# Row transposes of three chunks by transfers instead of TensorE, with the last steps of a spectral stage regrouped

## Chip, cores and metric

The kernel runs on one core of one Trainium2 chip. The metric is the device time of one execution in microseconds (us), the median of several runs. Before the change it is 183.4 us, the median of three runs between 183.24 and 183.43.

## What is computed

```python
def reference(A_x, A_w_r, A_w_i, B_x, B_w_gate, B_w_up, B_w_down):
    x = A_x                                   # 1 x 2048 x 512, bf16
    xn = _layernorm(x, axis=-1)
    # branch A: a filter in the frequency domain
    #   X = rfft2(xn) * (w_r + 1j*w_i);  y = irfft2(X)
    # branch B: a gated MLP, 512 -> 1792 -> 512
    #   h = gelu(xn @ w_gate) * (xn @ w_up);  z = h @ w_down
    return x + _A_ref(xn, A_w_r, A_w_i) + _B_ref(xn, B_w_gate, B_w_up, B_w_down)
```

B_x is not used. Both branches read the normalised rows xn.

## The kernel before

All work is written out by hand as a list of operations for each engine (PE is TensorE, ACT is ScalarE, DVE is VectorE, POOL is GpSimd, SP is SyncE). `sch.op(engine, fn, deps)` appends one operation; at its place in the list the engine waits for the semaphores in `deps` and goes on. So each engine, SP with its transfers too, works strictly in the order in which the Python code names the operations. Nearly all transfers are issued by SP, on one queue (q1) that is spread over 16 rings; six transfers (`back` with "act") and two early loads are issued by ScalarE on q10.

**Rows.** The 2048 rows are 16 row tiles of 128 (index j), four chunks of four tiles (512 rows). `ln_stats`, `ln_rstd` and `ln_apply` (L402 to L427) normalise a tile into `xn`, which lies in `bufA`. For the MLP the rows are needed transposed. `transposes(a, b, ring)` (L432) does this for tiles a to b-1: 16 transposing matmuls against the identity for a whole chunk (L444), into two PSUM banks, and two evictions into `xnT`, one on VectorE (L451) and one on ScalarE (L453). The first chunk is transposed in two halves before the loops; chunk two right before the loop over j, chunks three and four inside it.

**MLP.** `geglu_unit(b, fc)` ("g", L493) takes row chunk b and one of 14 column tiles: 4 matmuls with w_gate and 4 with w_up (L507), a gelu on ScalarE (L519) and a product on VectorE into `hT` (L527). `down_unit(b, jj)` ("d", L541) is 14 matmuls with w_down (L555) for one row tile, added to x on VectorE (L561). A list `fillers` holds all these units in order; `filler()` puts the next one into the program. They fill TensorE's time between the steps of branch A. Down units of chunk b-1 are put among the g units of chunk b at the positions in L789.

**Spectral branch.** The steps, in the order of the program:
- `half_fold` (POOL, L464) and `mirror_fold` (DVE, L471) form sums and differences of xn in `half` (in `bufC`) and `fold` (in `bufB`).
- Loop over j = 0 to 15 (L823): a filler, `unit_A(j)` (four matmuls, L577), `unit_d(j-1)` (four matmuls, L603). ScalarE evicts `unit_d` into `T[j]` (L611), which lies over `xn` in `bufA`, and SP stores `T[j]` to DRAM `stage_p` (L613; streams dr0 for j under 8, dr1 for the others). The dictionary `beside` names what else is put after each j. The filters wr and wi are loaded by SP at j = 1 and j = 5, ten transfers each (L339).
- `shuffle(q)` (L616): two transfers, SP, that bring half of `stage_p` back into `Tp` (in `bufC`) in another order; they wait for all stores of that half. shuffle(0) stands at j = 10, shuffle(1) after the loop. Every `unit_B` waits for both (`perm1`). `load_eg` (L393) follows, then five fillers.
- Loop over u = 0 to 18 (L842): `unit_c(u-4)`, `unit_B(u)`, `product(u-3)`, a filler. `unit_B` (two matmuls, L649) is evicted by ScalarE into `Xc` (L654), and SP copies it with the halves of the partitions swapped into `JX` (two transfers, L657). `product` (three VectorE operations, L666 to L668) multiplies by the filter. `unit_c` (two matmuls, L680) is evicted by ScalarE into `Vp` (L685), and SP stores it to DRAM `stage_g` (L689). At the end of this loop several c and products come together (L843, L848).
- `back(part, pq, eng)` (L692): transfers that return `stage_g` into `V` (in `bufB`), each waiting for the stores of its part, eight groups. Parts 0 to 2 are issued by ScalarE inside the loop, part 3 by SP after it.
- Five fillers, and a last loop: `unit_e(j)` (L711, needs all of V) evicted into `ZT` (L716, in `bufA`), `unit_fin(j)` (L732), and the sum into x, which SP stores to the output (L539).

The functions that the diff touches follow.

Of the kernel before, what the change touches and what calls it, by code (L numbers as in the profile page):

```python
# [151 lines left out]
class _Sched:  # L152
# [14 lines left out]
    def total(self, stream):  # L167
        return (stream, self.stream_cnt[stream])
# [59 lines left out]
def bass_parallel_sum__spectral_gfnet__glu_gated_geglu__prompt_kernel(  # L228
# [21 lines left out]
    with ExitStack() as es:  # L250
# [34 lines left out]
        xn = bufA[:, :].rearrange("p (j c) -> p j c", j=NJ)  # L285
        T = xn
        ZT = bufA[:, :].rearrange("p (ci j q) -> p ci j q", ci=4, j=NJ)

        fold = bufB[:, :].rearrange("p (t s j d) -> p t s j d", t=2, s=2, j=NJ)
        V = bufB[:, :].rearrange("p (j c) -> p j c", j=NJ)  # L290
# [28 lines left out]
        def sp_bank_bf(slot):  # L319
# [11 lines left out]
        streams += [(n, 16) for n in ("x0", "x1", "x2", "x3", "xc1", "xc2", "xc3", "ident", "small", "fa", "eg", "wd", "wr", "wi",  # L331
                                      "w0", "w1", "w2", "w3", "dr0", "dr1", "perm1", "jx0", "jx1", "jx2", "jx3", "vd0_0", "vd0_1", "vd0_2", "vd1_0", "vd1_1", "vd1_2", "vd2_0", "vd2_1", "vd2_2", "vd3_0", "vd3_1", "vd3_2", "perm2", "out")]
        for name, inc in streams:
# [95 lines left out]
        ev_xnT = {}  # L429
        tr = {}  # L430

        def transposes(a, b, ring, per=2):  # L432
# [23 lines left out]
            for j in range(a, b):  # L456
                ev_xnT[j] = evs
                tr[j] = ev_t

# [137 lines left out]
        def unit_d(j):  # L597
# [12 lines left out]
            src = sp_bank(slot).rearrange("p (h q m) -> p q h m", h=2, q=2)  # L610
            ev_T[j] = sch.op("act", lambda e: e.activation(dst, src, ACT.Copy), deps=[ev_p, tr[j]] + ev_hf[j // 4])  # L611
            ring_sp.add_reader(slot, ev_T[j])
# [92 lines left out]
        def unit_e(j):  # L705
# [9 lines left out]
            src = sp_bank(slot).rearrange("p (ci q) -> p ci q", ci=4)  # L715
            ev_ZT[j] = sch.op("act", lambda e: e.activation(ZT[:, :, j, :], src, ACT.Copy), deps=[ev_p] + [spec["dr%d" % q] for q in range(2)])  # L716
            ring_sp.add_reader(slot, ev_ZT[j])
# [68 lines left out]
        for b in range(4):  # L786
            units = [("g", b, fc) for fc in range(NHALF if b == 0 else 0, NFC)]
            if b >= 1:
                for n, at in enumerate((4, 7, 10, 13) if b < 3 else (3, 5, 7, 14)):  # L789
                    units.insert(at + n, ("d", b - 1, n))  # L790
            fillers += units
# [16 lines left out]
        for j in range(4, 8):  # L808
            ln_apply(j)
        filler(2)  # L810
        transposes(4, 8, ring_tr)
        half_fold(1)
# [4 lines left out]
            4: tuple((ln_apply, i) for i in range(8, 12)) + ((half_fold, 2),),  # L817
            5: ((ln_stats, 12), (ln_stats, 13), (transposes, 8, 12, ring_sp)), 6: ((ln_stats, 14), (mirror_fold, 2, 0)),
            7: ((ln_stats, 15), (ln_rstd, 12, 16), (mirror_fold, 2, 1)),
            8: tuple((ln_apply, i) for i in range(12, 16)) + ((half_fold, 3),), 9: ((transposes, 12, 16, ring_sp),),  # L820
            10: ((mirror_fold, 3, 0), (mirror_fold, 3, 1), (clear_holes,), (shuffle, 0)),
        }
        for j in range(NJ):  # L823
# [18 lines left out]
        for u in range(19):  # L842
            for v in ((14, 15) if u == 18 else (u - 4,)):  # L843
                if v >= 0:
                    unit_c(v)
            if u < 16:
                unit_B(u)
            for v in {16: (13, 14), 17: (15,), 18: ()}.get(u, (u - 3,)):  # L848
                if v >= 0:
                    product(v)  # L850
            if 1 <= u < 18:
                filler()

            if u in (9, 10, 13, 14, 17, 18):
                back(u // 4 - 2, (u - 9) % 4, "act")
        for pq in range(2):
# [61 lines left out]
```

## Time and profile before

| | us |
|---|---|
| median of three runs | 183.4 |
| the profiled execution's own time | 182.99 |
| its span in the profile | 181.2 |
| TensorE busy | 175.1 |
| VectorE busy | 117.3 |
| ScalarE busy | 88.5 |
| GpSimd busy | 55.5 |
| L444, transposing matmuls, 64 of them | 4.4 |
| L451 and L453, their evictions for whole chunks, 3 each | 2.0 and 3.1 |
| L613, the store of T[j], from issue to landing (median of 16) | 7.5 |
| L622, a shuffle transfer of 512 KB, from issue to landing (median of 4) | 5.1 |

The span runs from the first to the last recorded instruction. Busy time is the sum of an engine's instructions; the busy time of pipelined matmuls overlaps (64 transposing matmuls have 4.4 us but take less of the path). The chain of waits goes back from the last instruction, at each step to what released it, so what is on it lies on the path that sets the end. A DMA row gives the mean busy share of the 16 rings in tenths, one digit for each fortieth of the stretch.

### The profile page before, as it was taken

The numbers are of one execution on the slowest core, as the hardware profiler recorded it, in microseconds if no ns is written. First come the engines' busy times: TensorE is split into PE (matmuls) and PEld (weight loads), VectorE is DVE, ScalarE is ACT, GpSimd is POOL, SyncE is SP. The second block draws the span as 40 slices with busy tenths as digits, with TensorE's granted clock in tenths as the row PEclk, the third lists the DMA queues.
The fourth block names the chain that finished last, engine by engine and source line by source line (L and its number), as shares of the span: only waits on it lengthen the run. The fifth ranks groups of instructions, "written<-read, shape, count | busy, mean of one in ns | idle before, by whom it ended". The sixth has DMA issues, their size and how long they took to land.

```text
span 181.2 us, 3176 instructions
## 1 busy us (share of the span) xinstructions
PE 175.1 (97%) x1148; PEld 99.8 (55%) x1168; DVE 117.3 (65%) x252; ACT 88.5 (49%) x161; POOL 55.5 (31%) x54
## 2 busy tenths in 40 slices
PE   7889999999999999999999999999999999999994
PEld 7778555565655554455455554444555555555453
DVE  3758958799675545538678585933266758886431
ACT  2744357777463542166576574523363636663000
POOL 0082290373630000000000000000049679997900
PEclk9999999999999999999999999999999999999999
DMA  5999970999999585723436858475001121110101
GB/s 153 354 364 374 371 250 30 187 195 195 208 205 201 156 257 157 220 58 98 112 87 131 204 113 215 103 168 116 5 0 58 37 75 36 58 60 5 58 29 58
DMA packets 32224, 26.10 MB, mean 144 GB/s; under 512 B 2256, under 2 KB 31440, under 8 KB 32080
## 3 DMA queue, kind: packets, MB, share of 16 engines
q1 hardware_dynamic: 28368, 23.90, 50.2%
q10 hardware_dynamic: 3840, 2.00, 5.3%
q8 instruction: 9, 0.15, 0.4%
q14 instruction: 7, 0.06, 0.1%
HBM read 17.48 MB, written 6.30 MB: 131 GB/s over the span
## 4 chain that ended last, share of the span: by engine, by line
PE 90%; DMA 4%; DVE 3%; SPq 1%; issue 1%
PE ps L507 50%; PE ps L555 27%; DMA wu_sb<-in_B_w_up_dram 4%; PE ps L577 2%; PE ps L732 2%; PE ps L711 2%; PE ps L603 2%; PE ps L649 2%; PE ps L680 2%; PE ps L444 2%; SPq L339 1%; DVE hT L527 1%; DVE tmp L666 1%; DVE tmp L668 0%; DVE JX L667 0%
## 5 line engine op out<-in xcount | busy, mean ns | idle before, releaser
L507 PE MATMUL ps<-xnT,wu_sb 128*128 128x512 bf16 (+1 forms) x246 | 58.3, 358 | 0.1
L507 PE MATMUL ps<-xnT,wg_sb 128*128 128x512 bf16 (+1 forms) x234 | 56.2, 357 | 1.3 <-DMA wu_sb<-in_B_w_up_dram 0.5
L527 DVE TENSOR_TENSOR hT<-ps,gg 128x512 bf16<-128x512 f32 (+1 forms) x62 | 39.5, 638 | 21.7 <-PE ps L507 20.5
L555 PE MATMUL ps<-wd_sb,hT 128*128 128x512 bf16 (+1 forms) x234 | 50.3, 366 | 0.2
L519 ACT ACTIVATE gg<-ps 128x512 bf16<-128x512 f32 (+1 forms) x62 | 34.4, 555 | 25.4 <-PE ps L507 24.3
L746 POOL TENSOR_TENSOR bufC<-bufC 128x256 bf16<-128x256 f32 x16 | 14.7, 917 | 85.5 <-DVE bufC L743 85.5
L507 PEld LDWEIGHTS ps<-xnT,wu_sb 128*128 128x128 bf16 x248 | 24.2, 98 | 24.2
L555 PEld LDWEIGHTS ps<-wd_sb,hT 128*128 128x128 bf16 x238 | 22.9, 98 | 22.6
L507 PEld LDWEIGHTS ps<-xnT,wg_sb 128*128 128x128 bf16 x248 | 22.9, 98 | 16.0 <-DMA wu_sb<-in_B_w_up_dram 0.7
L561 DVE TENSOR_TENSOR x_sb<-ps,x_sb 128x512 bf16<-128x512 f32 (+1 forms) x17 | 11.2, 660 | 28.7 <-PE ps L555 28.7
L750 POOL TENSOR_TENSOR x_sb<-x_sb,bufC 128x512 bf16<-128x512 bf16 x16 | 18.7, 1170 | 2.3
L468 POOL TENSOR_TENSOR bufC<-bufA 128x1024 bf16<-128x1024 bf16 x8 | 16.8, 2125 | 7.9 <-DVE bufA L426 7.9
L611 ACT ACTIVATE bufA<-ps 128x512 bf16<-128x512 f32 x16 | 11.9, 744 | 9.2 <-PE ps L603 9.2
L685 ACT ACTIVATE Vp<-ps 128x514 bf16<-128x514 f32 x16 | 9.6, 599 | 13.6 <-PE ps L680 13.6
L716 ACT ACTIVATE bufA<-ps 128x512 bf16<-128x512 f32 x16 | 9.4, 597 | 13.5 <-PE ps L711 13.5
L403 DVE BATCH_NORM_STATS2 st<-x_sb 128x6 f32<-128x512 bf16 x16 | 10.9, 678 | 2.2 <-DMA x_sb<-in_A_x_dram 2.2
L742 DVE TENSOR_TENSOR bufC<-bufC,ps 128x256 f32<-128x256 f32 x16 | 6.7, 421 | 5.3 <-ACT bufC L739 5.3
L654 ACT ACTIVATE Xc<-ps 128x514 bf16<-128x514 f32 x12 | 7.0, 595 | 4.0 <-PE ps L649 4.0
L418 POOL TENSOR_SCALAR rstd<-ag 128x4 f32<-128x4 f32 (+1 forms) x4 | 1.6, 402 | 20.2 <-DVE ag L404 20.2
L584 ACT ACTIVATE tmp<-ps 128x512 bf16<-128x512 f32 x9 | 5.4, 597 | 4.5 <-PE ps L577 4.5
L739 ACT ACTIVATE bufC<-ps 128x256 f32<-128x256 f32 x16 | 6.0, 378 | 2.6 <-PE ps L732 2.6
L746 DVE TENSOR_TENSOR bufC<-bufC 128x256 bf16<-128x256 f32 x16 | 6.8, 425 | 0.5
(46 smaller groups left out, 144.1 us busy)
## 6 DMA issues: line engine op xcount, KB each, us to landing
stage_g<-Vp SPq DMA_DIRECT2D x16, 128.5 KB, 2.8
stage_p<-bufA SPq DMA_DIRECT2D x16, 128.0 KB, 7.5
bufC<-stage_p SPq DMA_DIRECT2D x4, 512.0 KB, 5.1
out_dram<-x_sb SPq DMA_DIRECT2D x15, 128.0 KB, 1.7
wd_sb<-in_B_w_down_dram SPq DMA_DIRECT2D x1, 1792.0 KB, 14.0
wr_sb<-in_A_w_r_dram SPq DMA_DIRECT2D x6, 257.0 KB, 6.5
wi_sb<-in_A_w_i_dram SPq DMA_DIRECT2D x6, 257.0 KB, 11.0
JX<-Xc SPq DMA_DIRECT2D x24, 64.2 KB, 2.3
```

The lines of the kernel that those rows point to most:

```text
L403: ev = sch.op("dve", lambda e: e.bn_stats(st[:, j, :], x_sb[:, j, :]), deps=[ev_x[j]])
L468: ev_hf[m] = [sch.op("pool", lambda e, t=t, op=op: e.tensor_tensor(half[:, m, t, :, :], rows[:, 0, :, :], rows[:, 1, :, :], op), deps=deps ...
L507: ins = e.matmul(gu_bank(slot)[:, 0:w], wsb[:, dc, fc * P:(fc + 1) * P], xnT[:, dc, b * 512 + a:b * 512 + a + w], start=(dc == 0), stop=(d ...
L519: ev_gg = sch.op("act", lambda e: e.activation(gg, gu_bank(gslot)[:, 0:w], ACT.Gelu_apprx_tanh), deps=[ev_gm] + gg_readers[s2])
L527: ev_h = sch.op("dve", lambda e: e.tensor_tensor(hT[hb][:, fc, a:a + w], gu_bank(uslot)[:, 0:w], gg, ALU.mult), deps=[ev_um, ev_gg] + hdeps)
L555: ins = e.matmul(bank(slot)[:, 0:w], hT[hb][:, fc, jj * P:(jj + 1) * P], wd_sb[:, fc, cs], start=(fc == 0), stop=(fc == NFC - 1))
L561: ev_a = sch.op("dve", lambda e, slot=slot, cs=cs: e.tensor_tensor(x_sb[:, j, cs], bank(slot)[:, 0:w], x_sb[:, j, cs], ALU.add), deps=[ev_ ...
L611: ev_T[j] = sch.op("act", lambda e: e.activation(dst, src, ACT.Copy), deps=[ev_p, tr[j]] + ev_hf[j // 4])
L685: ev_v = sch.op("act", lambda e: e.activation(Vp[sv][:], sp_pair(slot), ACT.Copy), deps=[ev_p] + Vp_readers[sv])
L716: ev_ZT[j] = sch.op("act", lambda e: e.activation(ZT[:, :, j, :], src, ACT.Copy), deps=[ev_p] + [spec["dr%d" % q] for q in range(2)])
L746: y = [sch.op(("dve", "pool")[h], lambda e, h=h, op=op: e.tensor_tensor(rS[s2][:, h * HD:(h + 1) * HD], yeS[s2][:, 0, :], yeS[s2][:, 1, :] ...
L750: ev_o = sch.op("pool", lambda e: e.tensor_tensor(x_sb[:, j, :], x_sb[:, j, :], rS[s2], ALU.add), deps=[a, b, ev_xn[j]] + ev_acc.get(j, []))
```

## The change

Chunks two to four (tiles 4 to 15) are no longer transposed by TensorE. A new `transfers(a, b)` has SP issue one transposing transfer per tile, from `xn` to `xnT`, 12 in all. Those of chunk two stand where their transposes stood; those of chunk three after j = 11, 12, 13 and 14; those of chunk four after u = 2, 4, 6 and 8 of the second loop. Since `xn` is now read later, `T` moves from `bufA` over `fold` in `bufB`, whose layout is turned so that the 512 elements of row tile j lie where `T[j]` is written. `T` no longer waits for the transposes and the half fold, and `ZT` (in `bufA`) waits for the transfers. The last down unit of chunk one moves from position 13 to 11 in the filler list. `product(13)` moves one step earlier (u = 15), 14 and 15 follow singly, `unit_c` 13 and 14 come together at u = 17 and 15 alone at u = 18. The third return (`back` of part 2) moves from u = 17 and 18 to u = 16 and 17.

```diff
-        T = xn
-        fold = bufB[:, :].rearrange("p (t s j d) -> p t s j d", t=2, s=2, j=NJ)
+        fold = bufB[:, :].rearrange("p (j t s d) -> p t s j d", t=2, s=2, j=NJ)
+        T = bufB[:, :].rearrange("p (j c) -> p j c", j=NJ)
...
+        def transfers(a, b):
+            for j in range(a, b):
+                sch.op("sp", lambda e, j=j: e.dma_start(xnT[:, :, j * P:(j + 1) * P], xn[:, j, :], transpose=True),
+                       deps=[ev_xn[j]], stream="tr%d" % (a // 4))
+                ev_xnT[j] = [total("tr%d" % (a // 4))]
+            for i in range(a // 4 * 4, b):
+                ev_xnT[i] = [total("tr%d" % (a // 4))]
...
-            ev_T[j] = sch.op("act", lambda e: e.activation(dst, src, ACT.Copy), deps=[ev_p, tr[j]] + ev_hf[j // 4])
+            ev_T[j] = sch.op("act", lambda e: e.activation(dst, src, ACT.Copy), deps=[ev_p])
...
-            ev_ZT[j] = sch.op("act", ..., deps=[ev_p] + [spec["dr%d" % q] for q in range(2)])
+            ev_ZT[j] = sch.op("act", ..., deps=[ev_p] + [ev_xnT[i][0] for i in (4, 8, 12)])
...
-                for n, at in enumerate((4, 7, 10, 13) if b < 3 else (3, 5, 7, 14)):
+                for n, at in enumerate(((4, 7, 10, 13), (4, 7, 10, 11), (3, 5, 7, 14))[b - 1]):
...
-        transposes(4, 8, ring_tr)
+        transfers(4, 8)
...
-            5: ((ln_stats, 12), (ln_stats, 13), (transposes, 8, 12, ring_sp)), 6: ((ln_stats, 14), (mirror_fold, 2, 0)),
-            7: ((ln_stats, 15), (ln_rstd, 12, 16), (mirror_fold, 2, 1)),
-            8: tuple((ln_apply, i) for i in range(12, 16)) + ((half_fold, 3),), 9: ((transposes, 12, 16, ring_sp),),
+            5: ((ln_stats, 12), (ln_stats, 13)), 6: ((ln_stats, 14), (mirror_fold, 2, 0)),
+            7: ((mirror_fold, 2, 1), (ln_stats, 15), (ln_rstd, 12, 16)),
+            8: tuple((ln_apply, i) for i in range(12, 16)) + ((half_fold, 3),),
...
+            11: ((transfers, 8, 9),), 12: ((transfers, 9, 10),), 13: ((transfers, 10, 11),), 14: ((transfers, 11, 12),),
...
-            for v in ((14, 15) if u == 18 else (u - 4,)):
+            for v in {17: (13, 14), 18: (15,)}.get(u, (u - 4,)):
                 if v >= 0:
                     unit_c(v)
...
-            for v in {16: (13, 14), 17: (15,), 18: ()}.get(u, (u - 3,)):
+            for v in {15: (12, 13), 16: (14,), 17: (15,), 18: ()}.get(u, (u - 3,)):
...
-            if u in (9, 10, 13, 14, 17, 18):
-                back(u // 4 - 2, (u - 9) % 4, "act")
+            if u in (2, 4, 6, 8):
+                transfers(11 + u // 2, 12 + u // 2)
+            if u in (9, 10, 13, 14, 16, 17):
+                back((u - 8) // 4, {16: 0, 17: 1}.get(u, (u - 9) % 4), "act")
```

## Prediction

> **What bounds the kernel now.** I read the page's first part, then the chain of waits in order of time, then the timelines of TensorE and SyncE, then the DMA rows of three stretches. The first two say that TensorE is the path.
>
> ```profile
> PE 175.1 (97%) x1148; PEld 99.8 (55%) x1168; DVE 117.3 (65%) x252; ACT 88.5 (49%) x161; POOL 55.5 (31%) x54
> ...
> PE 90%; DMA 4%; DVE 3%; SPq 1%; issue 1%
> ```
>
> The chain that ended last is 90% TensorE. Until about 10 us it is the loads, and from there to 178.8 us it is matmuls back to back, with one break. From the same chain, in order of time (start, length, what):
>
> ```profile
> 23.97 0.89 PE ps L444 x16
> ...
> 37.68 0.89 PE ps L444 x16
> ...
> 48.74 0.89 PE ps L444 x16
> ...
> 113.34 0.69 DVE hT L527
> ...
> 117.61 0.44 DVE tmp L668
> 118.09 0.40 PE ps L680 x2
> ```
>
> L444 is the transposes of row chunks two to four: three blocks of sixteen, each 0.89 us long, and all three stand on the path. The break is at 113 to 118 us, where the chain leaves TensorE for VectorE: the last two `unit_c` wait for the last two `product`.
>
> **Removed from TensorE.** 48 transposes, 3 x 0.89 = 2.67 us, with matmuls directly before and after each block: **-2.67**. Their evictions go too (three DVE copies of 0.67 us, three ACT copies of 1.02 us). Neither engine is the path there (DVE 65%, ACT 49%), so I count nothing for them; they were covered by matmuls and their going uncovers nothing.
>
> The Trainium skill, page "VectorE: DVE Perf Modes", section "The three transpose paths", gives 390 ns for a 128x128 bf16 transpose on TensorE and 1309 ns through the DMA crossbar, which speaks against this change. The first figure does not hold here (0.89/16 = 56 ns). No row shows the second; if a transfer of four blocks took 4 x 1.309 = 5.2 us of queue, four of them would take 21 us, which no slack below holds, and the kernel would be slower by well over 10 us.
>
> **The lag at the end.** From the start of unit c(12) at 113.14 us (TensorE's timeline) to the end of c(15) at 118.09 + 0.22, 5.17 us pass. The work in it is four `unit_c` of 0.22 and two fillers of 1.73, 4.34 us, so 0.83 us is idle. In the change `product(13)` stands one step earlier, and a down unit of 3.02 us lies at u = 16 where an up/gate unit of 1.73 lay. On VectorE, in the old clock: product 12 at 111.8, 13 at 112.9, the filler's multiply at 114.0, product 14 at 114.7 to 115.8. c(13) and c(14) come only at 113.36 + 3.02 = 116.4. Product 15 follows the down unit's addition (ends 117.2) and ends at 118.3; c(15) stands behind the next filler at 118.55. All are in time: **-0.83**. What is late next is the third return: ScalarE issues it at u = 16 and waits there until the stores of units 8 to 11 have landed (old clock about 114.8, ScalarE free at 114.2). Behind it in ScalarE's order is V(13), not due before 116.6, so the 0.6 us wait is covered by the down unit.
>
> The moved down unit is missing as cover between c(15) and the first `unit_e`. Before: 128.25 - 118.31 = 9.9 us, of which the returned V took until about 127 (last return issued at 123.1, median 3.8 to landing). After: five fillers of 1.73, 8.65 us from 118.77, so `unit_e` is due at 127.4 and V is there between 126.9 and 127.8, depending on how much the earlier third return relieves the queue. I take 0 and keep 0 to 0.4.
>
> **The added transfers.** Twelve transfers of 128x512 bf16, 128 KB each, on SP and its queue. The trace shows no transposing transfer. Two unknowns: T, the time that one takes of the 16 rings, and c, SP's time to issue one.
>
> T: the stage_p stores, 128 KB with rows of 1 KB, pass at up to 385 GB/s (DMA row of 64 to 74 us), 131072/385 = 0.34 us. The stretch of the filter loads, mostly rows of 514 bytes, moves 197 GB/s:
>
> ```profile
> 31.00:59.00 28.00, 27.78 (x211) 15.95 (x213) 21.11 (x43) 17.95 (x29) 11.62 (x8) 1.00 1.09 197
> ```
>
> that is 131072/197 = 0.67 us. A transposing transfer writes runs of 128 elements, 256 bytes, nearer to the second row, so I take T = 0.67; low end 0.34, high end twice the nearest row for half the run, 1.33. c: SP's rows run from 0.36 (stage_g) over 0.60 (JX, also SBUF to SBUF) to 2.35 us (the load of `small`, behind a full queue). I take 0.6. An issue price below zero is excluded, since each transfer is one more instruction.
>
> The Trainium skill, page "DMA: Bandwidth & Descriptors", section "Latency and other measured facts", states 261 GB/s for a DMA transpose, by which a transfer would take 0.50 us as an estimate, the stall below would be 1.1 and the time 181.0; no run shows it yet.
>
> *Chunk two* (four transfers behind xn(4..7), 21.9 to 22.9 us). SP has nothing to issue from 14.3 to 30.1. Rings from 24 to 34 us, a digit per 0.25 us:
>
> ```profile
> DMA  9999998310300000000000000003910992039999
> ```
>
> The wd load leaves them at about 26.0, and the first store comes at 30.7, after the change 0.89 earlier, 29.8. So 3.8 us are free and 4T = 2.7 fits. The first user, g(1,0), stands at 35.5 - 0.89 = 34.6. Cost 0; at T = 1.33 the filter loads behind are late by 5.3 - 3.8 = 1.5 us.
>
> *Chunk three* (j = 11 to 14). Here it collides. SP's timeline:
>
> ```profile
> 46.70 6.24 SPq L613 DMA_DIRECT2D stage_p<-bufA  x5
> 59.42 1.30 SPq L622 DMA_DIRECT2D bufC<-stage_p  x2
> 60.77 6.28 SPq L613 DMA_DIRECT2D stage_p<-bufA  x6
> 68.43 1.24 SPq L622 DMA_DIRECT2D bufC<-stage_p  x2
> ```
>
> shuffle(0) waits on SP for the stores behind the filter loads and goes out at 59.42, long after T(10) is ready. This is set by the queue, which starts 0.89 us earlier after the change, not 2.67: shuffle(0) at 58.5. Behind it, in order: six stores with the four transfers between them, and shuffle(1), which waits for all the stores. The rings from 64 to 74 us:
>
> ```profile
> DMA  9999999999410077000000035659999999999999
> ```
>
> The first burst, shuffle(0) and five stores, ends at about 66.6; the lone 77 is the last store, which landed at 68.43; then come shuffle(1) and the load of eg. After the change T(15) is ready 2.67 earlier (66.7 - 2.67 = 64.0), but the burst ends at 65.7 + 4T, the last store needs 0.3 more and 0.45 to land: 66.45 + 4T. By SP's issue the bound is 58.5 + 1.3 + 6 x 0.4 + 4c + 1.7 = 63.9 + 4c, less than that for c under about 1.3. From there shuffle(1) takes as before: 69.0 + 6.5 = 75.5 is its last landing, 7.1 us after 68.43. So `unit_B(0)` may start at 73.55 + 4T = 76.2. TensorE reaches it at 77.14 - 2.67 = 74.47. Before, the data was there 1.6 us early; now TensorE stands 4T - 0.92 = **+1.74 us** in order, with no filler placed between. This is the new wait that eats most of the gain.
>
> *Chunk four* (u = 2, 4, 6, 8). Per step of 2.17 us SP issues two JX transfers (1.10) and a store (0.37): 0.7 free, c = 0.6 fits, and with 1.2 it needs the next step too. JX behind a transfer lands T later; products 3 to 9 start 2 to 5 us after their JX landed (JX lands 2.2 us after issue, up to 4.9, and is used two to three steps later). Cost 0; the cover is gone at a delay over 2 us. First use at g(3,0), 30 us later.
>
> *Moves that cost nothing:* T in `bufB` instead of `bufA` and `fold` ordered by row: the same bytes, runs of 128 elements as before; each T(j) overwrites only what unit_A(j) has read. Bounds of the fold's write: none to a few tenths on eight DVE instructions of 0.67, under matmuls. ZT's new wait (transfers done by about 100 us) has ended 28 us before its first use.
>
> **Sum.** -2.67 - 0.83 + 1.74 = -1.76. Against the profiled execution's 182.99 (span 181.2, 1.8 around it) that is 181.2; it lay 0.4 under the median 183.4 of the three runs, so by the median 181.6.
>
> **Rivals.**
> *Nothing waits at B(0).* T at or under 0.34 (stall 0.4 or less) or the transfers slip beside shuffle(0): -3.1 to -3.5, 179.9 to 180.3. For it: the rings' row shows lulls in shuffle(0)'s ramp. Against: the queue takes transfers in order and it is full there.
> *Slow transfers, slower than before.* If a transposing transfer holds the rings longer than T = 1.1, the stall at unit_B(0) is 4 x 1.1 - 0.92 = 3.5 and takes the whole gain; from there every 0.1 costs 0.4, and above 0.95 chunk two adds its delay of the filter loads. At T = 1.33: 4.4 + 1.5 - 3.5 = +2.4, 185.8. The same comes from c over 1.7, since 63.9 + 4c + 7.1 - 74.47 = 3.5 there. For it: runs of 256 bytes, and two instructions' worth of work for one; against: every SP row but those behind a full queue is under 0.6 us.
> *Not a real transpose.* If the transfer fell apart into single elements, 65536 per transfer, it would cost hundreds of us. I see nothing for it but that the trace has no such row.
>
> **Chances.** Forecast (T 0.45 to 1.0, 180.7 to 183.0) 0.46; no wait (179.8 to 180.7) 0.24; within 0.2% of before, which is all a measurement can tell from no change, 0.06; slower by more 0.24 (most of it under 187, 0.02 far above). The range 179.9 to 185.0 leaves out the far half of the slow case and a little at the bottom. Faster 0.70, same 0.06, slower 0.24.
>
> **What would show it.** L444 with 16 matmuls and not 64; the break at 113 us gone from the chain; TensorE idle before L649's first matmul, released by a transfer bufC<-stage_p, near 1.7 us; a group xnT<-bufA on SP, x12, with its issue time near 0.6. Wrong, if that idle time is nothing or over 3 us, if g(1,0) or L711 waits for a transfer, or if products wait for JX.

## The result, and the profile after

The changed kernel takes 189.75 us (median of 4 runs, 189.16 to 190.41); the kernel before, run beside it, 183.32 (4 runs, 183.21 to 183.43). The ratio is 1.035, with a 95% interval of 1.032 to 1.039: 6.4 us slower, where the forecast was 181.6 and the range ended at 185.0. The profiled execution took 189.59 us with a span of 187.8 (before: 182.99 and 181.2), so the account below, made on the two profiled executions, has 6.6 us to explain.

The page's busy row, its row of granted clock, and the chain's share by engine, which answer to the first two lines of the prediction:

```profile
PE 175.8 (94%) x1101; PEld 98.2 (52%) x1120; DVE 115.4 (61%) x249; ACT 85.5 (46%) x158; POOL 55.1 (29%) x54
...
PEclk9999999999999999859999999999999999999999
...
PE 68%; DMA 12%; DVE 7%; POOL 5%; SPq 3%; issue 2%; ACT 1%; DVEq 0%
```

TensorE has 47 matmuls fewer on record and yet is busier by 0.7 us. The clock row says why: two slices of 4.7 us, from 75.1 to 84.5 us, read 8 and 5 where every slice of before reads 9. The chain that ended last is TensorE for 68% of the span, where it was 90%; DMA has risen from 4% to 12%. The kernel is no longer carried by one engine.

The chain now leaves TensorE at four places: from 34 to 53 us over VectorE and GpSimd (TensorE's idle time behind it is 0.17 us), from 69 to 80 us, from 101 to 112 us (a product that waits for JX) and from 126 to 135 us (the returned V). The second place and what follows it, in order of time (start, length, what), and below it the same step in the chain of the kernel before:

```profile
70.31 1.19 SPq L461
...
72.17 1.81 DMA stage_p<-bufB
74.00 0.55 SPq L629
74.59 5.74 DMA bufC<-stage_p
...
80.38 1.04 PE ps L656 x4
...
81.64 3.19 PE ps L514 x7
84.83 0.34 PE ps L656 x2
```

```profile
77.14 0.45 PE ps L649 x4
...
77.64 1.67 PE ps L507 x7
```

(L461 is the new transfer; L620 the store of `T`, L629 the shuffle, L656 `unit_B`, L514 the up/gate matmuls, L687 `unit_c`: what were L613, L622, L649, L507 and L680 before.) Up to 72 us the chain lies on SP, which issues stores and transfers in turn; then the last store lands, shuffle(1) goes out, and 6.4 us later `unit_B(0)` may start. Its four matmuls then take 1.04 us and the seven behind them 3.19, where before they took 0.45 and 1.67: half clock.

SP's own timeline of the same stretch, beside that of the prediction (start, length, line, number of DMAs issued):

```profile
22.00 5.90 SPq L461 DMA_TRANSPOSE xnT<-bufA  x4
...
59.80 1.30 SPq L629 DMA_DIRECT2D bufC<-stage_p  x2
61.15 1.37 SPq L620 DMA_DIRECT2D stage_p<-bufB  x1
62.56 1.30 SPq L461 DMA_TRANSPOSE xnT<-bufA  x1
63.90 1.92 SPq L620 DMA_DIRECT2D stage_p<-bufB  x1
65.87 1.91 SPq L461 DMA_TRANSPOSE xnT<-bufA  x1
67.83 0.58 SPq L620 DMA_DIRECT2D stage_p<-bufB  x1
...
71.55 1.05 SPq L620 DMA_DIRECT2D stage_p<-bufB  x2
74.00 1.25 SPq L629 DMA_DIRECT2D bufC<-stage_p  x2
```

The left-out rows are two transfers more (1.19 each) with a store of 0.58 between them. Each row starts where the last one ended: from 59.80 to 72.60 SP has no gap. A transfer occupies it for 1.19 to 1.91 us, a store for 0.4 to 1.92.

Where the 6.6 us arise, by four points on TensorE (the chain and TensorE's timeline of both executions):

| point | before | after | change in this stretch |
|---|---|---|---|
| `unit_B(0)` starts | 77.14 | 80.38 | +3.2: 2.67 saved, 5.7 waited, 0.2 of other shifts |
| `unit_B(2)` starts | 79.32 | 84.83 | +2.3: half clock |
| `unit_c(15)` ends (its start and 0.22) | 118.31 | 125.69 | +1.9: down unit moved in +1.29, idle of the lag gone -0.83, waits +1.4 |
| first `unit_e` starts | 128.25 | 134.78 | -0.9: the down unit no longer here -1.29, new wait +0.4 |
| end of span | 181.2 | 187.8 | +0.1 |

TensorE's rows of the waits in the last two stretches, all in the changed kernel (in brackets, the idle time before and what ended it):

```profile
109.44 0.40 PE L687 MATMUL ps<-tmp,small 128*128 128x257 bf16 x2 [0.48 <-DVE tmp L675]
...
112.10 0.40 PE L687 MATMUL ps<-tmp,small 128*128 128x257 bf16 x2 [0.32 <-DVE tmp L675]
...
134.78 0.62 PE L718 MATMUL ps<-fa,bufB 128*128 128x128 bf16 x8 [0.29 <-DMA bufB<-stage_g]
```

### The profile page after: what moved, and what is told of

Same layout as the page of the kernel before. It is cut to its first block, busy times and chain, and to the rows that moved or that the text cites. A ratio compares the mean times of both kernels' runs of the same rounds, so it can differ in the third digit from the quotient of the medians.

```text
span 187.8 us, 3089 instructions
## 1 busy us (share of the span) xinstructions
PE 175.8 (94%) x1101; PEld 98.2 (52%) x1120; DVE 115.4 (61%) x249; ACT 85.5 (46%) x158; POOL 55.1 (29%) x54
## 4 chain that ended last, share of the span: by engine, by line
PE 68%; DMA 12%; DVE 7%; POOL 5%; SPq 3%; issue 2%; ACT 1%; DVEq 0%
PE ps L514 37%; PE ps L562 21%; POOL bufC L475 4%; DMA bufC<-stage_p 3%; DMA JX<-Xc 2%; DMA bufB<-stage_g 2%; PE ps L718 2%; DMA stage_g<-Vp 2%; PE ps L739 2%; DVE bufA L426 2%; PE ps L656 2%; PE ps L687 2%; DMA x_sb<-in_A_x_dram 2%; SPq L461 1%; DVE hT L534 1%
## 5 line engine op out<-in xcount | busy, mean ns | idle before, releaser
L514 PE MATMUL ps<-xnT,wu_sb 128*128 128x512 bf16 (+1 forms) x246 | 59.1, 362 | 0.1
L514 PE MATMUL ps<-xnT,wg_sb 128*128 128x512 bf16 (+1 forms) x235 | 56.9, 360 | 1.0 <-issue 0.2
L514 PEld LDWEIGHTS ps<-xnT,wu_sb 128*128 128x128 bf16 x248 | 24.5, 99 | 24.8 <-issue 1.1
L514 PEld LDWEIGHTS ps<-xnT,wg_sb 128*128 128x128 bf16 x248 | 23.2, 99 | 16.2 <-issue 0.8
L618 ACT ACTIVATE bufB<-ps 128x512 bf16<-128x512 f32 x16 | 11.9, 743 | 9.6 <-PE ps L610 9.6
L723 ACT ACTIVATE bufA<-ps 128x512 bf16<-128x512 f32 x16 | 9.4, 597 | 13.9 <-PE ps L718 13.9
L656 PE MATMUL ps<-bufC,small 128*128 128x257 bf16 x32 | 6.6, 298 | 5.7 <-DMA bufC<-stage_p 5.7
L656 PEld LDWEIGHTS ps<-bufC,small 128*128 128x128 bf16 x32 | 3.3, 105 | 7.5 <-DMA bufC<-stage_p 6.2
## 6 DMA issues: line engine op xcount, KB each, us to landing
stage_g<-Vp SPq DMA_DIRECT2D x16, 128.5 KB, 3.6
```

What stands on the lines that cost most here:

```text
L514: ins = e.matmul(gu_bank(slot)[:, 0:w], wsb[:, dc, fc * P:(fc + 1) * P], xnT[:, dc, b * 512 + a:b * 512 + a + w], start=(dc == 0), stop=(d ...
L656: ins = e.matmul(sp_bank(slot + i)[:, 0:NK], BM[:, 1 if g == 0 else 0, :], Tp[:, g, :], start=True, stop=True)
```

## The experiments

After the result I had these theories. **S**: SP's issue of a transposing transfer, two to three times the price that I took, delays the last store of `T` and so shuffle(1). **R**: it is the added bytes on the rings. **C**: the wait at `unit_B(0)` is so long that the clock falls, which adds 2.3 us. **J**: chunk four's transfers delay JX in the second loop. A last one concerns the lag alone. Thirteen kernels ran, one of them twice. "Before" is the kernel before, run beside them; a time without an interval is a single execution. Kernels that ran ten or twelve times spread over 1.5 to 2.2 us, and TensorE's idle time in the first 14 us, where nothing was changed, lies between 1.3 and 2.8 us in the traces; so a difference of under 1 us between two single executions says little by itself.

**c3_plain: chunk three's transfers made plain.** The same four DMAs with the same bytes at the same places, but no transpose, so that the MLP of chunk three reads rows that aren't transposed (its output differs there).

```diff
+        def plain(a, b):
+            for j in range(a, b):
+                sch.op("sp", lambda e, j=j: e.dma_start(xnT[:, :, j * P:(j + 1) * P], xn[:, j, :].rearrange("p (r s) -> p r s", r=4)),
+                       deps=[ev_xn[j]], stream="tr%d" % (a // 4))
...
-            11: ((transfers, 8, 9),), 12: ((transfers, 9, 10),), 13: ((transfers, 10, 11),), 14: ((transfers, 11, 12),),
+            11: ((plain, 8, 9),), 12: ((plain, 9, 10),), 13: ((plain, 10, 11),), 14: ((plain, 11, 12),),
```

> The four transfers of chunk three (j = 11 to 14) copy the same bytes to the same places without transposing; so the MLP of chunk three reads rows that are not transposed. Theory S (SP's issue time of a transposing transfer, 1.2 to 1.9 us, delays the last store of T, and with it shuffle(1)): a plain copy is issued in 0.4 to 0.6 us, shuffle(1) goes out 3 to 4 us earlier than 74.0, TensorE's wait at unit_B(0) falls from 5.7 to 1.5 to 3 us, the clock stays at 1.0 and the time is 184 to 186. Rival R (the bytes on the rings behind shuffle(0) delay it): the same bytes in the same 256-byte runs, so shuffle(1) stays near 74.0, the wait at 5 to 6 us, the time at 189 to 190.

Measured 186.49 (before 183.23), 3.1 us less than the changed kernel and a little above S's range; shuffle(1) goes out 1.9 us earlier, not 3 to 4.

**c3_pe: chunk three back on TensorE**, the rest of the change kept.

```diff
+            5: ((ln_stats, 12), (ln_stats, 13), (transposes, 8, 12, ring_sp)), 6: ((ln_stats, 14), (mirror_fold, 2, 0)),
...
-            11: ((transfers, 8, 9),), 12: ((transfers, 9, 10),), 13: ((transfers, 10, 11),), 14: ((transfers, 11, 12),),
```

> Chunk three is transposed by TensorE again where it was before (0.89 us on the path); chunks two and four stay transfers. Theories S and R: no transfer lies between shuffle(0) and shuffle(1), so perm1 lands at 75.5 to 76 as before, TensorE comes to unit_B(0) at 75.4, waits 0 to 0.6 us, the clock stays at 1.0: 189.6 - 5.7 - 2.1 + 0.9 + about 0.3 = 182.5 to 183.5, with the waits for JX of about 1 us still there. Rival T (T in bufB or chunk two's transfers make the shuffles late): the wait stays above 3 us, 186 or more.

Measured 182.94 (before 183.23). Two rows of SP's timeline of the plain kernel, then TensorE's rows of the plain kernel and of that with chunk three on TensorE:

```profile
63.52 0.65 SPq L460 DMA_DIRECT2D xnT<-bufA  x1
...
72.13 1.27 SPq L636 DMA_DIRECT2D bufC<-stage_p  x2
```

```profile
78.63 0.62 PE L663 MATMUL ps<-bufC,small 128*128 128x257 bf16 x4 [3.11 <-DMA bufC<-stage_p]
```

```profile
76.96 0.62 PE L656 MATMUL ps<-bufC,small 128*128 128x257 bf16 x4 [1.18 <-DMA bufC<-stage_p]
```

The three kernels differ in chunk three alone, and `unit_B(0)` starts at 76.96 without its transfers, at 78.63 with plain copies and at 80.38 with transposing ones. So four plain copies of these bytes cost 1.7 us here, and the transposing form 1.75 more. Between the shuffles SP is occupied 3.0 us less with the plain form (60.68 to 70.44, against 59.80 to 72.60): 2.4 in the transfers, 0.6 in the stores. That the 1.75 is SP's issue and not slower rings is seen at the last store of `T`: by the trace's landings it lands 1.8 us after its issue in the changed kernel (72.17 to 73.99) and 2.1 in c3_plain (69.99 to 72.12), so it stays no longer in the queue; it is issued later. S holds for this half. For the 1.7 of the plain copies I cannot tell issue from bytes: without any of the four the last store lands 3.2 us after its issue (66.67 to 69.91, c3_pe), so there it is the queue that sets shuffle(1).

In the second loop c3_plain waits 1.53 us for a product, and 0.65 at the first `unit_e`. c3_pe waits for no product, though chunk four goes by transfers in it and I had expected about 1 us there. Its 1.18 at `unit_B(0)`, with no transfer between the shuffles, lies above the 0 to 0.6 that I had expected; it comes back below.

**warm: the clock held up.** 80 multiplications of the identity ahead of `unit_B(0)`, into a bank that nobody reads.

```diff
+        def f_w(e):
+            ins = None
+            for i in range(80):
+                ins = e.matmul(bank_of(7)[:, 0:P], ident, ident, start=True, stop=True)
+            return ins
+        sch.op("pe", f_w, deps=bdeps)
```

> After as it is, with 80 small matmuls (identity by identity, into a free bank, about 4.5 us) on TensorE directly ahead of unit_B(0), where it waits 5.7 us. Theory C (the idle time itself makes the granted clock fall to 0.5 for 4.4 us afterwards, which costs 2.1 us): unit_B(0) still starts at 80.4, the clock is 1.0 from there on, the time is 187.3 to 187.9. Rival: the clock falls for another reason, or the price is none: 189.3 to 190.

Measured 189.93 (before 183.23): nothing gained, against my expectation. TensorE's timeline of this kernel:

```profile
75.95 4.64 PE L855 MATMUL ps<-small 128*128 128x128 bf16 x80 [0.79 <-DVE x_sb L568]
80.76 0.62 PE L656 MATMUL ps<-bufC,small 128*128 128x257 bf16 x4 [0.17 <-DMA bufC<-stage_p]
...
111.89 0.40 PE L687 MATMUL ps<-tmp,small 128*128 128x257 bf16 x2 [2.21 <-DVE tmp L675]
```

The clock is whole (the stretch behind has 1.00 where the changed kernel has 0.50, and `unit_B` takes 0.62 and not 1.04), but the time comes back as waits: 2.21 us in the second loop, where a product waits for its JX (the changed kernel waits 0.80 there), 0.81 at the first `unit_e` (for 0.29), and `unit_B(0)` starts 0.4 later. The half clock and the late JX lay side by side: mending one uncovers the other.

**c4_pe and c4_warm: chunk four back on TensorE**, once as it is and once with 62 such multiplications.

```diff
+            8: tuple((ln_apply, i) for i in range(12, 16)) + ((half_fold, 3),), 9: ((transposes, 12, 16, ring_sp),),
...
-            if u in (2, 4, 6, 8):
-                transfers(11 + u // 2, 12 + u // 2)
```

> After, with chunk four on TensorE again (its 0.89 us fall into the wait at unit_B(0)); chunks two and three stay transfers. Theory: unit_B(0) still starts near 80.4 at half clock, which costs 2.1 us; the second loop, rid of four transfers of 1.28 us each on SP, has no wait for JX: 188 to 188.8. Rival (the second loop's waits come from elsewhere): 189.3 or more.

> The same with 62 small matmuls (identity by identity, into a free bank) ahead of unit_B(0), so that TensorE is not idle there. Theory C (the clock's fall costs 2.1 us, and the earlier trial gained nothing only because SP and the queue bounded the second loop): the clock stays at 1.0 and the time is 2.0 us under the kernel without them, 186 to 186.8. Rival (the half clock costs nothing that the loop does not wait for anyway): the same time as without them.

Measured 187.78, a little under what I had expected, and 186.10 (before 183.13). The stretches of 4.4 us from `unit_B(0)` on, for the first and the second kernel (columns: stretch, length, busy time and instructions of TensorE, its weight load, VectorE, ScalarE and GpSimd, granted clock, DMA share, GB/s):

```profile
80.80:85.20 4.40, 4.40 (x18) 2.13 (x19) 0.69 (x1) 2.15 (x4) 0.00 (x0) 0.69 0.26 71
```

```profile
80.10:84.50 4.40, 4.29 (x23) 2.36 (x25) 0.70 (x2) 2.88 (x5) 0.00 (x0) 1.00 0.37 110
```

The clock is 0.69 in the first and 1.00 in the second. From `unit_B(0)` to `unit_B(2)` they take 3.51 and 2.18 us, so of the 1.7 us between the two kernels 1.3 is the clock; `unit_B(0)` also starts 0.64 earlier, and 0.3 of the two is lost again later. Neither waits for JX in the second loop. Theory C holds where the second loop is not the limit: with the late JX gone the clock is worth 1.3 us, with it there it is worth nothing. And chunk four's transfers, which I had at nothing, are worth 3.8 us between the two kernels with a whole clock (189.93 to 186.10, 0.6 of it an earlier `unit_B(0)`) and 1.8 between the two without it (189.59 to 187.78), where 0.9 of it is a shorter spell of half clock.

**c4_only: chunk four alone by transfers** (two and three on TensorE, the loop's end as before).

```diff
-        transfers(4, 8)
+        transposes(4, 8, ring_tr)
...
+            5: ((ln_stats, 12), (ln_stats, 13), (transposes, 8, 12, ring_sp)), 6: ((ln_stats, 14), (mirror_fold, 2, 0)),
...
-            11: ((transfers, 8, 9),), 12: ((transfers, 9, 10),), 13: ((transfers, 10, 11),), 14: ((transfers, 11, 12),),
```

> Only chunk four by transfers (u = 2, 4, 6, 8), chunks two and three on TensorE, the end of the loop as before. Theory: 0.89 us off the path, perm1 at 75.5 still 0.7 us ahead of TensorE at unit_B(0): 182.3 to 182.6, ratio 0.995. Rival J (waits for JX and the V stores eat it): 183 to 183.6.

Measured 183.56 (6 runs; before 183.03), ratio 1.003 [1.001, 1.004]. SP's timeline in the kernel before and in this one over the same steps, and the wait that follows:

```profile
96.40 0.37 SPq L689 DMA_DIRECT2D stage_g<-Vp  x1
96.89 1.10 SPq L657 DMA_DIRECT2D JX<-Xc  x2
```

```profile
97.08 1.27 SPq L461 DMA_TRANSPOSE xnT<-bufA  x1
98.39 0.59 SPq L696 DMA_DIRECT2D stage_g<-Vp  x1
99.09 1.11 SPq L664 DMA_DIRECT2D JX<-Xc  x2
100.24 0.59 SPq L696 DMA_DIRECT2D stage_g<-Vp  x1
```

```profile
105.76 0.40 PE L687 MATMUL ps<-tmp,small 128*128 128x257 bf16 x2 [1.23 <-DVE tmp L675]
```

Before, a store and two JX take 1.47 us of a step of 2.17 and SP then rests. With a transfer in every second step, two steps need 1.27 + 2 x 0.59 + 2 x 1.11 = 4.67 us of SP, and they last 4.34: SP falls behind and has no gap left. `unit_c` then waits 1.23 us for a late JX, more than the 0.89 that the chunk saves. Theory J holds here. The JX that is waited for is the pair issued at 99.09, in the kernel before at 96.89. By the trace's landings it takes 5.7 us, and before 5.3, with 2.1 us to spare; counted from `unit_B(0)` it is issued 3.2 us later. So of the lateness 3.2 us are SP's and 0.4 the queue's. In both kernels this pair goes out while the first return, issued by ScalarE, is under way; the pairs before it land in 2.5 to 3.5 us in the kernel before.

The price is not a fixed one. With chunk four at the same steps, the traces of c3_pe and best1 show no wait of TensorE for a late JX, and those of c3_late and c3_early 0.70 and 0.87.

**lag_only: the end of the second loop alone** (last lag, down unit, third return; all transposes on TensorE, `T` in `bufA`). The edit takes the kernel before and puts in only the hunks of `product`, `unit_c`, the position 11 and `back`.

```diff
-                for n, at in enumerate((4, 7, 10, 13) if b < 3 else (3, 5, 7, 14)):
+                for n, at in enumerate(((4, 7, 10, 13), (4, 7, 10, 11), (3, 5, 7, 14))[b - 1]):
...
-            for v in {16: (13, 14), 17: (15,), 18: ()}.get(u, (u - 3,)):
+            for v in {15: (12, 13), 16: (14,), 17: (15,), 18: ()}.get(u, (u - 3,)):
```

> Before, with only the regrouped end of the second loop, the moved down unit and the third return (no transfers). Theory: the idle 0.83 us at 113 to 118 us goes, unit_e then waits 0 to 0.4: 182.5 to 182.9, a ratio of 0.995 to 0.998. Rival: the wait moves whole to unit_e, since the down unit is missing as cover there: 183.2 to 183.6, ratio 1.000.

Measured 183.64 (12 runs; before 183.23), ratio 1.001 [0.999, 1.003]. TensorE no longer waits for a product, and waits further down:

```profile
128.56 0.62 PE L711 MATMUL ps<-fa,bufB 128*128 128x128 bf16 x8 [0.87 <-DMA bufB<-stage_g]
```

The 0.83 us went whole to the first `unit_e`. `unit_c(15)` ends at 118.9, 0.6 later than before, because the down unit now lies ahead of it; the last of V lands 9.6 us after it (128.5), where before it landed 8.9 us after it (127.2).

**c3_early, c3_late and c3_only: chunk three's transfers elsewhere.** The first sends all four ahead of shuffle(0); the second behind the load of `eg`, which follows shuffle(1). Both keep the rest of the change. The third puts them between shuffle(1) and `eg`, with chunks two and four on TensorE and the old end.

In all three the line with (transfers, 8, 9) to (transfers, 11, 12) goes. Then, for c3_early, c3_late and c3_only in turn:

```diff
-            10: ((mirror_fold, 3, 0), (mirror_fold, 3, 1), (clear_holes,), (shuffle, 0)),
+            10: ((mirror_fold, 3, 0), (mirror_fold, 3, 1), (clear_holes,), (transfers, 8, 12), (shuffle, 0)),
```

```diff
         load_eg()
+        transfers(8, 12)
```

```diff
+        transfers(8, 12)
         load_eg()
```

> After, with the four transfers of chunk three ahead of shuffle(0), where SP sits idle from 52 to 60 us, and none between the shuffles. Theory S (it is SP's issue time between shuffle(0) and shuffle(1) that costs most): the issue hides in the idle time, the rings owe 4 x 0.62 = 2.5 us of which 1.4 fall into the lull before shuffle(0); shuffle(1) goes out at 70 to 71.5, TensorE waits 1.5 to 3 us at unit_B(0), the clock stays at 1.0, 183.5 to 185.5. Rival R (bytes on the rings ahead of shuffle(1), wherever they are put): the wait stays at 4 us or more, 187 or more.

> After, with the four transfers of chunk three behind shuffle(1) and the load of eg, where SP has nothing to issue until unit_B(0). Both theories: perm1 lands as with chunk three on TensorE (76 to 77 us), TensorE comes 0.89 earlier (74.5) and waits 1.5 to 2.4 us, so 182.5 to 183.5, no better than with chunk three on TensorE. This tells whether the path up to unit_B(0) is now the chain of transfers: if so, the 0.89 us that TensorE saves is lost in the wait. Rival: the time falls by the 0.89, 181.8 to 182.2.

> Only chunk three by transfers, behind shuffle(1) and ahead of eg; chunks two and four on TensorE, the old end of the loop. Theory: 0.89 us off the path and the second loop untouched: 182.1 to 182.5, ratio 0.995. Rival: eg and the first JX copies, pushed back by 5 us of SP's time, make product(0) late: 182.8 to 183.3.

Measured: early 185.65, late 183.9 (before 183.03), only 183.11 (10 runs; before 183.08), ratio 1.001 [0.999, 1.003]. TensorE's waits in the three, in this order:

```profile
77.70 1.04 PE L656 MATMUL ps<-bufC,small 128*128 128x257 bf16 x4 [2.90 <-DMA bufC<-stage_p]
```

```profile
76.37 0.62 PE L656 MATMUL ps<-bufC,small 128*128 128x257 bf16 x4 [1.54 <-DMA bufC<-stage_p]
...
80.02 1.04 PE L514 MATMUL ps<-xnT,wg_sb 128*128 128x512 bf16 x4 [1.08 <-DMA xnT<-bufA]
```

```profile
78.97 1.04 PE L514 MATMUL ps<-xnT,wg_sb 128*128 128x512 bf16 x4 [0.59 <-DMA xnT<-bufA]
...
83.43 0.40 PE L687 MATMUL ps<-tmp,small 128*128 128x257 bf16 x2 [0.62 <-DVE tmp L675]
```

Ahead of shuffle(0), behind the filter loads, the four hold SP for 8.2 us (53.26 to 61.47) and shuffle(0) goes out at 61.59. The wait of 2.90 was expected, the fall of the clock behind it (1.04 for four matmuls) was not. Late, the transfers no longer delay the shuffle, but the up/gate matmuls of chunk three come before the transfers have landed. Between shuffle(1) and `eg` the shuffle is in time and the transfers nearly so, but the first JX, which the first product needs, is late instead: behind the transfers and `eg` it is issued 2.6 us after `unit_B(0)` (before: 1.0) and takes 4.1 us to land (before: 2.6). In each place what the chunk saves is given back; none of the three beats before.

**best1 and best2: chunks three and four in the places that seemed free.** best1: chunk two on TensorE, chunk three behind `eg`, chunk four as in the change, old end. best2: chunk two on TensorE, chunk three between shuffle(1) and `eg`, chunk four at u = 1, 3, 5, 7.

> Chunk two on TensorE, chunk three by transfers behind the load of eg, chunk four by transfers at u = 2, 4, 6, 8, the end of the second loop as before the change. Theory: no transfer is ahead of the filter loads or between the shuffles, so perm1 lands at 74.6 to 75.5 and TensorE, 1.78 us earlier, comes to unit_B(0) at 75.4: a wait of 0 to 0.3, 181.5 to 182.3, ratio 0.990 to 0.995. Rival J (the transfers at u = 2 to 8 make products wait for JX and the V stores, or the chain of returned V bounds unit_e): 182.5 to 183.5.

> As the version with chunk two on TensorE and the old end of the loop, but chunk three's transfers now directly behind shuffle(1) and ahead of the load of eg (they were waited for 0.87 us behind it), and chunk four's at u = 1, 3, 5, 7, so that the last is through before the first return starts at u = 9. Theory: 48 - 16 = 32 transposing matmuls leave the path, 1.78 us, with no new wait: 181.3 to 182.0, ratio 0.990 to 0.995. Rival J (SP is so full in the second loop that JX or the V stores come late whatever the place): 182.7 to 183.3.

Measured 183.25 (10 runs; before 183.03), ratio 1.003 [1.001, 1.005], and 183.95 (12 runs; before 183.08), ratio 1.004 [1.002, 1.006]: both slower than before by 0.3 to 0.4%, and best2 above the ranges of theory and rival. best1 has no wait at `unit_B(0)` (75.79) but one of 0.87 for chunk three's transfers; best2 one of 0.49 for these and one of 0.58 at the first product, as in c3_only. Later in the second loop neither trace has a wait for JX over 0.13 us, so chunk four costs nothing there in these two. But the two traces are of executions faster than the medians (182.88 and 183.34), and best1's ten fall into two groups, six from 182.85 to 183.37 and four from 183.93 to 184.39. What the slower ones wait for is not shown.

best1 measures T on the way: its four transfers go out one behind another with nothing in between, 1.3 to 1.6 us apart, and by the trace's landings they end at 77.67, 78.16, 78.66 and 79.18, so 0.50 us of rings each.

**c2_only and c2_again: chunk two alone**, chunks three and four on TensorE, the old end; run twice, the second time with six executions.

```diff
+            5: ((ln_stats, 12), (ln_stats, 13), (transposes, 8, 12, ring_sp)), 6: ((ln_stats, 14), (mirror_fold, 2, 0)),
...
+            8: tuple((ln_apply, i) for i in range(12, 16)) + ((half_fold, 3),), 9: ((transposes, 12, 16, ring_sp),),
...
-            11: ((transfers, 8, 9),), 12: ((transfers, 9, 10),), 13: ((transfers, 10, 11),), 14: ((transfers, 11, 12),),
...
-            if u in (2, 4, 6, 8):
-                transfers(11 + u // 2, 12 + u // 2)
```

> Only chunk two by transfers, the others on TensorE, the old end of the loop. Theory: the transfers land at 28 to 32 us and push the filter loads behind them back by about 1 us, so shuffle(0) goes out at 60.3 instead of 59.4 and perm1 lands at 76.2 to 76.8; TensorE, 0.89 earlier at 76.2, waits 0 to 0.6 us: 182.8 to 183.4, nothing gained. Rival: they lie in the idle stretch of the rings and cost nothing: shuffle(0) at 58.5 to 59.4 and 182.2 to 182.5.

> Only chunk two by transfers, the others on TensorE, the old end of the loop, measured again in rounds against the kernel before. Theory: TensorE's 0.89 us come through, since SP is idle from 14 to 30 us and unit_B(0) keeps 0.2 us of slack: ratio 0.994 to 0.997, 182.1 to 182.6. Rival (the single look was luck): 0.998 to 1.002.

Measured 182.13 (before 183.08), then 182.17 (6 runs, 181.93 to 182.43; before 183.13, 11 runs), ratio 0.9945 [0.9927, 0.9963]: **faster than the kernel before by 0.96 us, 0.5%.** My theory of that time had said that nothing would be left; the rival, an idle stretch, was nearly right in the time, though shuffle(0) went out at 60.29 and not by 59.4. Of the second, SP's row of the four transfers and TensorE's of `unit_B(0)`, then TensorE's of the kernel before:

```profile
22.18 6.17 SPq L461 DMA_TRANSPOSE xnT<-bufA  x4
```

```profile
76.12 0.61 PE L656 MATMUL ps<-bufC,small 128*128 128x257 bf16 x4
```

```profile
76.98 0.61 PE L649 MATMUL ps<-bufC,small 128*128 128x257 bf16 x4
```

The 6.17 us lie where SP has nothing else to issue. `unit_B(0)` starts at 76.12 without a wait, 0.86 earlier than before, and the last of shuffle(1) landed at 76.04 (before: 75.50). The slack of 1.5 us that the kernel before had at this place, by these rows, is used up, from both sides. With chunk two on TensorE and nothing but stores between the shuffles, the last of shuffle(1) lands at 75.1 to 75.7 us by the trace's landings (before, lag_only, c4_only, c3_only, best1, best2); with chunk two by transfers at 75.8 to 76.9 (c2_only, c2_again, c3_late, c3_pe). The two groups lie close together, and all are single executions. This is where the 1.18 us of c3_pe come from: TensorE, with chunk four's 0.89 saved too, is there at 75.78, the data at 76.91, the latest of the four. Once chunk two goes by transfers, what else is saved ahead of `unit_B(0)` cannot be cashed there.

## Why the prediction was wrong

The step that failed first is the bound by SP's issue, "63.9 + 4c", which the prediction set aside for the rings' bound. Three of its terms were too small: a transposing transfer took SP 1.40 us and not 0.6, a store 0.92 and not 0.4, and shuffle(0) went out 1.3 us later. SP, not the rings, set the last store of `T`. After it come a cost that had no term, the half clock behind the long wait (2.3 us), and chunk four's "Cost 0" (1.4 us).

**Right: what TensorE saves.** It reaches `unit_B(0)` at 80.38 - 5.72 = 74.66 us; 74.47 was predicted from the 2.67.

**Right: where the new wait stands, and what ends it.** It is at `unit_B(0)`, ended by bufC<-stage_p. Its size failed, 5.72 us for 1.74.

**Right, and better than assumed: T.** 0.50 us of rings per transfer (best1), where I took 0.67. The skill's figure that the prediction cited (the Trainium skill, "DMA: Bandwidth & Descriptors", "Latency and other measured facts", 261 GB/s, by which a transfer takes 0.50 us as an estimate) agrees with that. The stall of 1.1 that follows from it does not: the rings were not the limit.

**Right: chunk two.** It costs no time and keeps its 0.89 (c2_again), but not quite as worked out: its transfers land at 29.5 to 32.4 us there, later than the 29.8 by which they were to be through, and the last of shuffle(1) lands 0.5 later than before. The slack at `unit_B(0)` covers it.

**Failed: the start of `unit_B(0)`, 76.2 for 80.38.** The prediction's steps, against the changed kernel:

| step | predicted | measured | off |
|---|---|---|---|
| shuffle(0) goes out | 58.5 | 59.80 | +1.3 |
| to shuffle(1), without transfers | 7.95 | 9.36 (c3_pe) | +1.4 |
| what the four transfers add to it | 4T = 2.68 | 4.84 | +2.2 |
| shuffle(1) to `unit_B(0)` | 7.1 | 6.38 | -0.7 |

The sum is +4.2. The first step said that the queue, and with it shuffle(0), starts 0.89 earlier. It does not: with chunk two on TensorE shuffle(0) goes out at 59.2 to 60.2 (before, c4_only, c3_only, lag_only, best1, best2), with its transfers at 59.8 to 60.9 (c3_early, which puts more ahead of it, apart). The second step let the stretch between the shuffles shrink to 7.95 because T(15) is ready earlier; in the eleven kernels with nothing but stores between the shuffles it lasts 8.4 to 9.6 us. In the kernel before and in lag_only the last store goes out as soon as T(15) is ready and lands 1.7 us later. In the other nine T(15) is ready 0.9 to 2.3 us earlier, but the store goes out up to 2.9 us after it and lands 2.7 to 3.8 us after its issue: SP and the queue set it, and the earlier T(15) gains nothing. The third is the step that I had worked out and put aside: "By SP's issue the bound is ... 63.9 + 4c, less than that for c under about 1.3", with c = 0.6 taken from SP's plain DMAs. c is 1.28 in the median of twelve (1.19 to 1.91), and the six stores take 0.4 to 1.92 where I had 0.4. With these, SP's bound stands above the rings': 59.80 + 1.30 + 5.59 for four transfers + 5.50 for six stores + 0.4 of gaps = 72.6, and the last store lands at 74.0. Against my 66.3 by SP's issue (63.9 and 4 x 0.6) the start is 1.3 late, the transfers 3.2 and the stores 3.1. The stores were mis-sized apart from the transfers: six in a row take SP 4.6 us in c3_early, where none of them had to wait for its T. c3_plain shows what the transposing form adds: the same bytes with c near 0.6 (three of four) bring `unit_B(0)` 1.75 us earlier. My range for c ended at 2.35, but by the sum SP's bound passed the rings' only from 1.3 and took the whole gain only from 1.7.

**Failed: no term for the clock.** +2.3 us (the table's second row). No wait of the kernel before was long enough to show it in its trace.

**Failed: "Cost 0" for chunk four.** It allowed for c = 1.2 with "it needs the next step too", but not that the stores behind a transfer rise from 0.37 to 0.59 and that two steps together are then over-full (c4_only). +1.4 us of waits in the second loop, nearly all of it from 108.8 to 114.4 us: two waits for JX, 0.48 and 0.32 by the timeline, and the short gaps around them.

**Failed: the lag's -0.83.** The idle time at `unit_c` went as worked out, but the step "five fillers of 1.73 ... I take 0 and keep 0 to 0.4" did not hold: V needs 8.9 to 9.6 us from the end of `unit_c(15)`, and the fillers cover 8.65, so lag_only waits 0.87 at `unit_e`, all that was gained. In the changed kernel 0.4 of it shows (0.29 of it one idle time, the rest short gaps).

Sum: 181.2 + 4.2 + 2.3 + 1.4 + 0.4 + 0.1 at the end of the span = 189.6, against 189.59 measured. These are the shares of this one execution. They are not prices that can be taken off singly: with the clock mended the second loop takes its share back (warm), and with chunk four back on TensorE the clock's share is 1.3 (c4_warm).

**The rivals.** "Slower than before" named slow rings first, and that is refuted (T = 0.50). Its second branch, SP's issue, was the mechanism, at a lower price than its point of decision: 1.40 for these four was enough because the stores and the late shuffle(0) had taken the slack already. No wait at `unit_B(0)`, and a transfer that falls apart, are refuted too.

**Open.** What makes a store behind a transfer slower to issue in the second loop (0.59 for 0.37); why one or two of the six stores between the shuffles take 1.1 to 1.8 us even without transfers, and with it how much of the longest transfer (1.91) is a full queue and not its own price; and why chunk four's transfers make JX late in some kernels and not in others.

## What to carry to other kernels

A DMA has two prices, its bytes on the rings and its time on the engine that issues it; work out both, and do not take the issue time of a transposing DMA from plain ones. Work taken off the bound engine is cashed only up to the slack of the next thing that it waits for: here 1.5 us ahead of `unit_B(0)`, which one chunk with its side effects uses up. Ask of each part by itself which resource is idle where it is put; of three chunks only the one that met an idle SP (22 to 28 us) was a gain, and 40 us later the same four instructions cost more than they saved.

## What the runs showed of the hardware

**Issue time of a transposing transfer.** 1.19 us at least for 128x512 bf16 on SP, 1.26 to 1.32 in the second loop of c4_only, 2.05 in the mean behind the filter loads (8.21 for four, c3_early), against 0.60 to 0.65 for three of the four plain copies of the same bytes. The twelve transfers add 6,500 packets to the page's count, some 540 each.

**The clock after a wait.** TensorE's clock read 0.50 in the stretch behind idle times of 2.90 (c3_early) and 5.72 us (the changed kernel), 0.69 over 4.40 us behind 5.52 (c4_pe), and 1.00 behind 3.11 (c3_plain). So the length of the wait alone does not decide. The rows of the changed kernel, of c3_early and of c3_plain:

```profile
80.40:84.80 4.40, 4.18 (x12) 1.92 (x14) 0.00 (x0) 1.69 (x3) 0.00 (x0) 0.50 0.31 92
```

```profile
77.70:80.40 2.70, 2.47 (x8) 1.32 (x10) 0.00 (x0) 1.09 (x2) 0.00 (x0) 0.50 0.15 47
```

```profile
78.60:81.00 2.40, 2.31 (x13) 1.35 (x15) 0.00 (x0) 1.69 (x3) 0.00 (x0) 1.00 0.31 120
```

The granted clock in the traces also shows when it changed. It fell at 78.13 us in the changed kernel, 77.14 in c3_early and 80.14 in c4_pe, that is 3.5, 2.3 and 4.9 us into the idle time, and stayed at half for 6.83, 3.41 and 3.41 us.

The Trainium skill, page "TensorE: Matmul & The Clock Gate", section "What's actually happening", states that the gate looks at a free-running window of 3413 ns and drops to half rate after an idle one. The half rate agrees with the 0.50, and the lengths of the half clock with one and two such windows. A window whose phase is not the kernel's would explain why the fall comes at different points of the idle time and why 3.11 us passed once; that the clock fell after 2.3 us of idle in c3_early, less than such a window, does not fit its figure.
